# A fused convolution and feed-forward block: the first matmul wholly in seven products, in two passes, with its sums and its output moved between engines and groups

## The chip, the cores and the metric

The kernel runs on 1 core of one Trainium2 chip. The metric is device microseconds (us) of one execution. Before the change three runs took 971.06, 972.87 and 970.63 us, median 971.06 us. PE is the matrix engine, DVE the vector engine, ACT the scalar engine, POOL is GpSimd, and SP issues most loads and stores.

## The reference, cut to what matters

```python
# x: (8, 4224, 192) f32; weight: (8 heads, 7 taps)
w = softmax(weight, axis=-1)
y[b, s, h*24 + g] = sum over k of w[h, k] * x_pad[b, s + k, h*24 + g]   # 6 zero rows ahead
mu, var = mean and variance of y over its 192 channels
yn = (y - mu) / sqrt(var + 1e-6) * g_ln
out = y + maximum(yn @ w_ch1, 0) @ w_ch2          # w_ch1: 192 x 768, w_ch2: 768 x 192
```

The mean and g_ln are folded into w_ch1 at the start. The factor 1/sqrt(var + 1e-6) is positive, so it goes through the maximum and is applied to the result of the second matmul.

## The kernel before, in words

**Groups.** The 33,792 rows are cut into 18 groups (line 70). Groups 0 to 2 are smaller and take the plain path; groups 3 to 17 have 16 rows on each of 128 partitions, and these "mixed" groups are nearly the whole run. A group goes through the same steps, spread over three turns of the main loop (line 912). Its x is loaded two turns ahead (`load_x`). Behind it the convolution `y` is made: tap 0 by ACT (`first_tap`, line 383), tap 1 by ACT into a scratch tile `tb` that two DMAs of POOL add to `y` (`second_tap`, lines 394 and 397), taps 2 to 6 by DVE (`conv`, line 408, 40 instructions, one for each tap and head). DVE then turns `y` into 32x32 transposed blocks `yt` (line 419) and takes the moments (line 439, 16 instructions).

**First matmul (`up_mixed`, line 584).** The 768 columns of w_ch1 are six chunks of 128, three in the left half (e = 0) and three in the right (e = 1). `yt` is cut in quarters a11 to a22 (two halves of the rows by two halves of the channels) and w1 in quarters b11 to b22, and the four result quarters c11 to c22 come from seven products in place of eight, at the price of sums of quarters: of w1 once (`sums_of_quarters`), of `yt` in each group (`sums_of_y`, lines 574 to 578, four DVE additions). Four of the six chunks go so, two at a time, each product into one of two sets of four PSUM banks, `chain` and `other`. The remaining two (`plain`) are made with all eight. ACT copies a finished product out of PSUM (`evict`, line 607). Where a second product has to be added to a quarter (`close`), ACT copies it into a scratch tile and a DMA of POOL adds it in SBUF (line 582); only in the last group DVE adds it straight from PSUM (line 614). The scratch tiles are taken from the pools of `tb` and of `cs`.

**Second matmul (`down_fast`, line 743).** Again seven products, here called A to G in their order, each of three columns and each column evicted by ACT (line 768). E, F and G read sums of hidden quarters that DVE makes between them (`half_sum`, line 727, nine instructions), and B reads a sum made by `lower_sum` (line 736, three instructions). Results gather in the tile `cs`; one of the two last additions is a DMA of POOL (`close_by_dma`), the other is DVE's (line 822).

**Output.** `finish_fast` transposes `cs` back into the tile `ot` (line 824, six instructions), at the end of the group's own turn. In the next group's first matmul ACT scales the 16 rows of `ot` by the root (line 849), and POOL issues two DMAs that add rows 0 to 7 and 8 to 15 to the output in DRAM (`add_to_out`, line 856), where SP has stored `y` before.

**What sets the order.** The schedule is manual: each engine runs its instructions in the order of the program text, and waits are put in where one instruction needs another. The pools of `yt`, `tb`, `cs`, `ot` and of the hidden tile have one buffer each (lines 106 to 112), so a new tile of such a pool waits until every reader of the last one is done, a DMA that reads it included. `x` and `y` have two buffers. DMAs that POOL issues share one queue.

Of the kernel before, what the change touches and what calls it, by code (L numbers as in the profile page):

```python
# [16 lines left out]
def kernel(  # L17
# [200 lines left out]
    def split_words(raw, mant, power, clamp=nc.vector):  # L218
        hi = raw[:, :, 1]
        nc.vector.tensor_single_scalar(mant.bitcast(U32), hi, 0xFFFFF, op=ALU.bitwise_and)  # L220
        nc.scalar.activation(mant.bitcast(F32), mant, AF.Relu, scale=2.0**-20, bias=1.0)
        nc.vector.tensor_scalar(
            out=power.bitcast(U32), in0=hi, scalar1=20, scalar2=0x7FF,
            op0=ALU.logical_shift_right, op1=ALU.bitwise_and,
        )
        clamp.tensor_scalar(  # L226
            out=power, in0=power, scalar1=896.0, scalar2=1151.0, op0=ALU.max, op1=ALU.min
        )
        nc.scalar.activation(power, power, AF.Relu, scale=float(1 << 23), bias=low)  # L229
# [46 lines left out]
    w1sums = consts.tile([P, 4, CH, PAIR * P], F32, name="w1sums")  # L276
# [88 lines left out]
    split_words(*words_a, nc.gpsimd)  # L365
    split_words(*words_b, nc.gpsimd)
    tap_matrices(range(3, K))
    join_words(w1f[:, 0:2].rearrange("p s f -> p (s f)"), *words_a, ga)
    join_words(w1f[:, 2], *words_b, gb)
# [143 lines left out]
    def rows_of_tiles(banks, left, right, first=True, last=True):  # L513


        chunks, w = right.shape[2] // P, left.shape[1] * left.shape[3]
        for c in range(left.shape[2]):
            for i in range(chunks):
                for q in range(NQ):
                    rows = slice(C * q, C * q + C)  # L520
                    nc.tensor.matmul(  # L521
                        banks[:, q, i * w : i * w + w], right[rows, c, P * i : P * i + P],
                        left[rows, :, c, :], start=(first and c == 0 and i == 0),
                        stop=(last and c == left.shape[2] - 1), skip_group_check=chunks > 1,
                    )
# [22 lines left out]
    def quarters_of_w1():  # L548
        return [
            w1[:, CH * k : CH * k + CH, P * f : P * (f + PAIR)] for k in range(2) for f in (0, FC)  # L550
        ]

    def sums_of_quarters(dst, b11, b12, b21, b22):

        for v, a, b in ((0, b12, b11), (1, b22, 0), (2, b12, b22), (3, b21, 1)):
            a, b = (dst[:, u] if isinstance(u, int) else u for u in (a, b))
            nc.vector.tensor_tensor(dst[:, v], a, b, op=ALU.subtract)
# [10 lines left out]
    def sums_of_y(g):  # L568

        room = upool.tile([P, 3 * HJ * CH * C], F32, tag="ys", name=f"ysums{g}")  # L570
        room = room.rearrange("p (v j c t) -> p v j c t", v=3, c=CH, t=width(g))
        ysums[g] = s1, s2, s3 = [room[:, v] for v in range(3)]
        a11, a12, a21, a22 = quarters_of_y(g)
        nc.vector.tensor_tensor(s1, a21, a22, op=ALU.add)
        nc.vector.tensor_tensor(s2, s1, a11, op=ALU.subtract)
        nc.vector.tensor_tensor(s3, a21, a11, op=ALU.subtract)
        yield
        nc.vector.tensor_tensor(s2, a12, s2, op=ALU.subtract)
        yield
# [4 lines left out]
    def up_mixed(g, last_sum):  # L584
# [4 lines left out]
        assert groups[g][2] == 2 * HJ and PAIR * W == 512  # L589
# [3 lines left out]
        b11, b12, b21, b22 = quarters_of_w1()  # L593
        s1, s2, s3 = ysums[g]
        (c11, c12), (c21, c22) = [
            [a[:, h, e, 0:PAIR].rearrange("p f q j t -> p f q (j t)") for e in range(2)]
            for h in range(2)
        ]
# [5 lines left out]

        def evict(banks, dst, relu=False, i=slice(0, PAIR)):
            src = banks.rearrange("p q (f w) -> p f q w", w=W)[:, i]
            nc.scalar.activation(dst, src, AF.Relu) if relu else nc.scalar.copy(dst, src)  # L607

        def close(c, banks, part, i=slice(0, PAIR)):


            if last:
                src = banks.rearrange("p q (f w) -> p f q w", w=W)[:, i]
                nc.vector.tensor_tensor(c[:, i], c[:, i], src, op=ALU.add)
                return
            evict(banks, part, i=i)
            whole = "p f q w -> p (f q w)"
            add_by_dma(c[:, i].rearrange(whole), part.rearrange(whole))

        def plain(f, banks):  # L620
            rows_of_tiles(banks, yt[g][:, 0 : 2 * HJ], w1[:, :, f * P : f * P + P])
            evict_up(g, f, banks)


        chain, other = take_set(), take_set()
        turn[0] += 4
        done = groups[g - 1][2]
        rooms = parts(bpool, "tb"), parts(cpool, "cs")
        first, second = (r[:, 0:PAIR] for r in rooms)
# [8 lines left out]

        rows_of_tiles(chain, a11, b11, True, False)
        evict(chain, c11)  # L640
        rows_of_tiles(other, a12, b21)
        close(c11, other, first)
        rows_of_tiles(chain, s2, w1sums[:, 1], False, False)
        evict(chain, c21)
        act_scales(0, 1)
        taps_of_next(2, 3)
        next(last_sum)
# [8 lines left out]
        rows_of_tiles(other, s3, w1sums[:, 2], True, False)  # L656
        evict(other, c22)
        act_scales(1, 2)
        rows_of_tiles(chain, s1, w1sums[:, 0], False, False)
        close(c22, chain, second)  # L660
        act_scales(2, 3)
        rows_of_tiles(other, a22, w1sums[:, 3], False)
        for i, room in enumerate(rooms):
            close(c21, other, room[:, PAIR : PAIR + 1], slice(i, i + 1))
        act_scales(3, 4)
        rows_of_tiles(chain, s2, b22, False)
        evict(chain, c12, True)
        nc.scalar.activation(c11, c11, AF.Relu)
        act_scales(4, 7)
        taps_of_next(3, 6)  # L670
        taps_of_next(6, K, heads=(0, H // 2))
        plain(PAIR, other)
        nc.scalar.activation(c22, c22, AF.Relu)
        if not last:
            scale(g - 1, 7, 10)
            add_to_out(g - 1, 0, 8)
        lower_sum(g, (PAIR,))
        lower_sum(g, range(PAIR))
        taps_of_next(6, K, heads=(H // 2, H))
        plain(PAIR + FC, chain)  # L680
        if last:

            rest = a[:, 1, 0, 0:PAIR, :, fast[g] :]
            for f in range(PAIR):
                nc.scalar.activation(rest[:, f], rest[:, f], AF.Relu)
        else:
            scale(g - 1, 10, done)
            add_to_out(g - 1, 8, done)
# [54 lines left out]
    def down_fast(g):  # L743
# [7 lines left out]
        part = cpool.tile([P, CH, NFAST * T], F32, tag="part", name=f"part{g}")[:, :, 0:w]  # L751
        part = part.rearrange("p c (j t) -> p c j t", t=t)

        parts = [part, a[:, 1, 0].rearrange("p f q j t -> p (f q) j t")[:, 0:CH]]
# [22 lines left out]
        def close_by_dma(c, part):  # L777
            add_by_dma(*(v.rearrange("p c j t -> p c (j t)") for v in (c, part)))

# [5 lines left out]
        taps_behind = [1, 4, 4, 7, 0, 0]  # L785
        product(0, a[:, 0, 0], b[0], c11, True)
        some_taps(taps_behind[0])
        product(1, a[:, 1, 0], w2sums[:, 2], c22, True)
        some_taps(taps_behind[1])
        product(1, a[:, 1, 1], w2sums[:, 3], parts[0], False)  # L790
        some_taps(taps_behind[2])
        product(1, a[:, 0, 1], b[2], None, True)
        some_taps(taps_behind[3])
        if g + 1 < NG:
            transpose(g + 1)
            moments(g + 1, 0, EARLY)
# [8 lines left out]
        product(0, a[:, 1, 1], w2sums[:, 1], c21, False)  # L805
        if g + 1 == NG:
            finish_fast(g, 0, flat, cs, parts)
        else:
            close_by_dma(c21, parts[0])
        some_taps(taps_behind[4])  # L810
        product(0, a[:, 0, 0], w2sums[:, 0], parts[1], False)
        some_taps(taps_behind[5])
        product(0, a[:, 0, 1], b[3], c12, False)
        some_taps(len(todo))
        return flat, cs, parts

    def finish_fast(g, half, flat, cs, parts):
        n = fast[g]
        ot = ots[g] if half else out_tile(g)
        if half or g + 1 == NG:  # L820
            fresh = cs[:, CH * half : CH * half + CH, 1]
            nc.vector.tensor_tensor(fresh, fresh, parts[half], op=ALU.add)
# [88 lines left out]
    store_y(0)  # L911
    for g in range(NG):
# [3 lines left out]
        if mixed:  # L916
            up_mixed(g, later)
        else:
            up(g)
        if not fast[g]:  # L920
# [13 lines left out]
            if g == 1:  # L934
                finish(0)
                root(0)
                sums_of_quarters(w2sums, *quarters_of_w2())
# [3 lines left out]
            elif g == 2:  # L941
                sums_of_quarters(w1sums, *quarters_of_w1())
                later = sums_of_y(3)
# [6 lines left out]
        parts = down_fast(g)  # L950

        if not last:
            moments(g + 1, EARLY)
            if g + 1 in MIXED:
                later = sums_of_y(g + 1)
                next(later)
            for half in range(2):
                finish_fast(g, half, *parts)
# [4 lines left out]
        else:  # L963
            finish_fast(g, 1, *parts)
            add_and_store(g, slice(0, fast[g]))
            down(g)
            finish(g)
# [30 lines left out]
```

## Time and profile before

| what | value |
|---|---|
| time of the profiled execution | 971.06 us |
| its span, first to last instruction | 969.3 us |
| around the span | 1.8 us |
| start of the first matmul of groups 3, 4, 5, ... 17 | 122.5, 178.7, 234.7, ... 906.4 us: 56.0 us each |
| of these: first matmul, second matmul | 28.64 and 27.33 us |
| from group 17's first matmul to the span's end | 62.8 us |

The span is what lies between the first and the last recorded instruction. Rows of the timeline give the start, the time from the first start to the last end, engine, line, operation, tiles, shape and count, and in brackets the engine's idle time before it and what ended that. In a table of stretches an engine's entry is its busy time and its number of instructions.

### The profile page before, as it was taken

The numbers are of one execution on the slowest core, as the hardware profiler recorded it, in microseconds if no ns is written. First come the engines' busy times: TensorE is split into PE (matmuls) and PEld (weight loads), VectorE is DVE, ScalarE is ACT, GpSimd is POOL, SyncE is SP. The second block draws the span as 40 slices with busy tenths as digits, with TensorE's granted clock in tenths as the row PEclk, the third lists the DMA queues.
The fourth block names the chain that finished last, engine by engine and source line by source line (L and its number), as shares of the span: only waits on it lengthen the run. The fifth ranks groups of instructions, "written<-read, shape, count | busy, mean of one in ns | idle before, by whom it ended". The sixth has DMA issues, their size and how long they took to land.

```text
span 969.3 us, 36017 instructions
## 1 busy us (share of the span) xinstructions
PE 956.9 (99%) x16194; PEld 672.8 (69%) x16194; DVE 870.0 (90%) x1487; ACT 640.3 (66%) x1014; POOL 205.3 (21%) x357
## 2 busy tenths in 40 slices
PE   6999999999999999999999999999999999999997
PEld 6886585857658585766758586675857667685767
DVE  6999999898998989899997989899798989989837
ACT  5725677585867858595876858587685858675351
POOL 3005310411123111411114011321104111130400
PEclk9999999999999999999999999999999999999999
DMA  8243888687796969789696978969697886766121
GB/s 205 93 134 123 173 199 234 127 161 230 147 271 127 247 124 190 206 156 271 128 247 125 194 198 152 266 132 249 132 216 176 147 255 133 178 123 111 28 59 68
DMA packets 29960, 163.17 MB, mean 168 GB/s; under 512 B 3567, under 2 KB 9839, under 8 KB 22126
## 3 DMA queue, kind: packets, MB, share of 16 engines
q0 software_dynamic: 22704, 97.53, 53.7%
q1 hardware_dynamic: 6798, 63.34, 17.0%
q8 instruction: 127, 2.08, 0.9%
q14 instruction: 27, 0.22, 0.1%
q10 hardware_dynamic: 304, 0.00, 0.0%
HBM read 38.95 MB, written 50.33 MB: 92 GB/s over the span
## 4 chain that ended last, share of the span: by engine, by line
PE 98%; DMA 1%; DVE 1%; POOL 0%; ACT 0%; issue 0%; SPq 0%
PE ps L521 49%; PE ps L762 41%; PE ps L707 6%; DMA room<-in_moe_w_ch_dram 1%; PE ps L320 1%; POOL room L226 0%; PE ps L344 0%; PE ps L349 0%; DVE y L863 0%; PE ps L329 0%; PE ps L332 0%; DVE room L245 0%; DVE room L237 0%; ACT room L229 0%; DVE ot L888 0%; DVE room L220 0%
## 5 line engine op out<-in xcount | busy, mean ns | idle before, releaser
L408 DVE SCALAR_TENSOR_TENSOR y<-xg,taps,y 128x384 f32<-128x384 f32 (+3 forms) x734 | 368.2, 581 | 1.4 <-issue 0.9
L521 PE MATMUL ps<-yt,w 32*128 32x256 f32 (+3 forms) x3744 | 287.7, 458 | 0.0
L521 PEld LDWEIGHTS ps<-yt,w 32*128 32x128 f32 x3744 | 187.9, 185 | 91.2 <-issue 81.0
L762 PE MATMUL ps<-room,w2sums 128*32 128x256 f32 (+1 forms) x4320 | 233.9, 375 | 0.0
L762 PEld LDWEIGHTS ps<-room,w2sums 128*32 128x32 f32 x4320 | 142.4, 110 | 86.0
L762 PE MATMUL ps<-room,w 128*32 128x256 f32 (+1 forms) x3240 | 179.9, 375 | 0.0
L727 DVE TENSOR_TENSOR room<-room 128x1024 f32<-128x1024 f32 (+1 forms) x135 | 151.4, 1196 | 9.7 <-ACT part L768 9.7
L762 PEld LDWEIGHTS ps<-room,w 128*32 128x32 f32 x3240 | 105.2, 110 | 73.4 <-ACT ot L849 10.6
L768 ACT COPY cs<-ps 128x256 f32<-128x256 f32 (+1 forms) x180 | 63.0, 366 | 97.7 <-PE ps L762 97.0
L607 ACT COPY room<-ps 128x2048 f32<-128x2048 f32 x45 | 84.0, 1867 | 55.1 <-PE ps L521 54.4
L521 PE MATMUL ps<-ysums,w1sums 32*128 32x256 f32 x2160 | 119.6, 374 | 0.0
L521 PEld LDWEIGHTS ps<-ysums,w1sums 32*128 32x128 f32 x2160 | 110.5, 185 | 6.4 <-ACT parts_tb L607 0.3
L824 DVE STREAM_TRANSPOSE ot<-cs 128x512 f32<-128x512 f32 (+1 forms) x90 | 55.9, 672 | 56.8 <-DMA cs<-part 34.5
L511 ACT ACTIVATE room<-ps 128x2048 f32<-128x2048 f32 (+3 forms) x46 | 71.3, 1549 | 33.6 <-PE ps L521 33.6
L849 ACT ACTIVATE ot<-ot,r 128x192 f32<-128x192 f32 x232 | 90.9, 448 | 0.0
L383 ACT ACTIVATE y<-xg,taps 128x384 f32<-128x384 f32 (+3 forms) x141 | 73.3, 589 | 6.9 <-DMA out_dram<-y 6.9
L856 POOL DMA_DIRECT2D out_dram<-ot x40 | 34.2, 1083 | 198.7 <-ACT ot L849 137.1
L439 DVE BATCH_NORM_STATS2 st<-y 128x6 f32<-128x192 f32 x264 | 71.0, 342 | 0.0
L397 POOL DMA_DIRECT2D y<-tb x28 | 24.6, 1036 | 176.2 <-ACT cs L768 172.8
L736 DVE SCALAR_TENSOR_TENSOR room<-room 128x1024 f32<-128x1024 f32 (+1 forms) x45 | 51.5, 1201 | 8.4 <-ACT room L509 7.6
L394 ACT ACTIVATE tb<-xg,taps 128x384 f32<-128x384 f32 x112 | 58.1, 604 | 0.0
L419 DVE STREAM_TRANSPOSE yt<-y 128x3072 f32<-128x3072 f32 (+3 forms) x19 | 56.2, 2957 | 1.9
(104 smaller groups left out, 796.3 us busy)
## 6 DMA issues: line engine op xcount, KB each, us to landing
xg<-in_x_dram SPq DMA_DIRECT2D x15, 2112.0 KB, 15.2
out_dram<-ot POOLq DMA_DIRECT2D x29, 768.0 KB, 8.0
y<-tb POOLq DMA_DIRECT2D x28, 768.0 KB, 9.5
out_dram<-y SPq DMA_DIRECT2D x13, 1536.0 KB, 10.5
room<-parts_tb POOLq DMA_DIRECT2D x14, 1024.0 KB, 7.4
room<-parts_cs POOLq DMA_DIRECT2D x14, 1024.0 KB, 7.1
room<-parts_tb POOLq DMA_DIRECT2D x14, 512.0 KB, 9.2
room<-parts_cs POOLq DMA_DIRECT2D x14, 512.0 KB, 10.8
```

Source lines behind the costliest of these rows:

```text
L383: nc.scalar.mul(y[g][:, 0:n, cs], xg[g][:, 0:n, cs], taps[:, h, 0:1])
L394: nc.scalar.mul(tb[g][:, 0:n, cs], xg[g][:, 1 : 1 + n, cs], taps[:, h, 1:2])
L408: nc.vector.scalar_tensor_tensor(out=y[g][:, 0:n, cs], in0=t[:, k : k + n, cs], scalar=taps[:, h, k : k + 1], in1=y[g][:, 0:n, cs], op0=AL ...
L439: nc.vector.bn_stats(out=sums[g][:, j, :], in_=y[g][:, j, :])
L511: nc.scalar.activation(dst, src, AF.Relu)
L521: nc.tensor.matmul(banks[:, q, i * w : i * w + w], right[rows, c, P * i : P * i + P], left[rows, :, c, :], start=(first and c == 0 and i = ...
L607: nc.scalar.activation(dst, src, AF.Relu) if relu else nc.scalar.copy(dst, src)
L707: nc.tensor.matmul(bank[C * q : C * q + C, 0:w], w2[:, f, C * c : C * c + C], left, start=(f == 0), stop=(f == NF - 1),)
L727: nc.vector.tensor_tensor(a[:, *dst, f], a[:, *left, f], a[:, *right, f], op=op)
L762: nc.tensor.matmul(dst[C * q : C * q + C, 0:w], right[:, f, C * c : C * c + C], left[:, f, q], start=(first and f == 0), stop=(f == FC - 1 ...
L768: nc.scalar.copy(to[:, c], dst[:, 0:w].rearrange("p (j t) -> p j t", t=t))
L849: nc.scalar.mul(ots[g][:, j, :], ots[g][:, j, :], rstd[g][:, j : j + 1])
```

## The change

The first matmul makes all six chunks with seven products, in two passes: pass one has one chunk of each half (7 products of 12 matmuls), pass two the other two (7 products of 24). The sums of w1 now span three chunks and are arranged so that one is kept in w1 itself. Two of the four sums of `yt` go to GpSimd, right behind the transpose; a fourth one overwrites a quarter of `yt`. In pass two the last addition to c21 is DVE's, from PSUM. In the second matmul the addition by DMA becomes DVE's, and `finish_fast` of a group stands in the next group, behind pass one and ahead of the taps. The scaling of `ot` is spread over pass two and the second matmul of the next group (`ending`), and the ACT taps of `first_tap` and `second_tap` are given out as 4, 6 and 6 behind the products C, D and E. At the start the bound on the exponents of w_ch1 goes from GpSimd to DVE.

```diff
-        clamp.tensor_scalar(
+        nc.vector.tensor_scalar(
             out=power, in0=power, scalar1=896.0, scalar2=1151.0, op0=ALU.max, op1=ALU.min
         )
...
+    def sums_of_y(g, engine):
...
+        engine.tensor_tensor(s3, a21, a11, op=ALU.subtract)
+        engine.tensor_tensor(s2, s3, a22, op=ALU.add)
         yield
-        nc.vector.tensor_tensor(s2, a12, s2, op=ALU.subtract)
+        nc.vector.tensor_tensor(s4, a12, s2, op=ALU.subtract)
+        nc.vector.tensor_tensor(a21, a21, a22, op=ALU.add)
...
+            def close(self, c, banks, part=None):
+                if part is None or last:
+                    nc.vector.tensor_tensor(c, c, self.seen(banks), op=ALU.add)
+                    return
+                self.evict(banks, part)
...
+        X, Y = take_set(), take_set()
+        one, two = Pass(PAIR, FC, X, Y), Pass(0, PAIR, Y, X)
+        room1 = parts(bpool, "tb")
+        p = one
+        p.product(X, a11, p.b11, True, False)
+        p.evict(X, p.c11)
+        p.product(Y, a12, p.b21)
+        p.close(p.c11, Y, room1[:, 0:1])
+        p.product(X, s2, p.t[0], False, False)
+        p.evict(X, p.c21)
+        p.product(Y, s3, p.t[1], True, False)
+        p.evict(Y, p.c22)
+        p.product(X, s1, p.b12, False, False)
+        p.close(p.c22, X, room1[:, 1:2])
+        p.product(Y, a22, p.t[2], False)
+        p.close(p.c21, Y, room1[:, 2:3])
+        p.product(X, s4, p.b22, False)
+        p.evict(X, p.c12, True)
+        next(ahead)
+        p = two
+        room2 = parts(cpool, "cs")
+        room3 = parts(bpool, "tb")
...
+        p.product(Y, s1, p.b12, False, False)
+        taps_of_next(2, 5)
+        taps_of_next(5, 6, heads=(0, H // 2))
+        p.close(p.c22, Y, room3[:, 0:PAIR])
+        p.product(X, a22, p.t[2], False)
+        taps_of_next(5, 6, heads=(H // 2, H))
+        p.relu(p.c11)
+        p.close(p.c21, X)
+        p.product(Y, s4, p.b22, False)
+        p.evict(Y, p.c12, True)
         lower_sum(g, (PAIR,))
         lower_sum(g, range(PAIR))
+        taps_of_next(6, K)
+        def ending(step):
+            if step == 0:
+                two.relu(two.c22)
+            if last:
+                return
+            cuts = [min(j, done) for j in (3, 6, 10, 13, J)]
+            if step < len(cuts) - 1:
+                scale(g - 1, cuts[step], cuts[step + 1])
+            if step == 1:
+                add_to_out(g - 1, 0, 8)
+            if step == 3:
+                add_to_out(g - 1, 8, done)
...
         product(0, a[:, 0, 0], b[0], c11, True)
+        ending(0)
         product(1, a[:, 1, 0], w2sums[:, 2], c22, True)
+        ending(1)
+        product(1, a[:, 1, 1], w2sums[:, 3], c21, False)
+        some_taps(4)
         product(1, a[:, 0, 1], b[2], None, True)
+        some_taps(6)
         if g + 1 < NG:
             transpose(g + 1)
-            moments(g + 1, 0, EARLY)
+            sums = sums_of_y(g + 1, nc.gpsimd)
+            next(sums)
+            moments(g + 1)
...
-        product(0, a[:, 1, 1], w2sums[:, 1], c21, False)
-            close_by_dma(c21, parts[0])
+        product(0, a[:, 1, 1], w2sums[:, 1], parts[0], False)
+        some_taps(6)
+        ending(2)
         product(0, a[:, 0, 0], w2sums[:, 0], parts[1], False)
+        some_taps(len(todo))
+        ending(3)
         product(0, a[:, 0, 1], b[3], c12, False)
+        if g + 1 < NG:
+            next(sums)
```

`next(ahead)` runs `finish_fast(g - 1, half, ...)` for both halves, the two calls that stood behind `down_fast`.

## The prediction

> **What bounds the kernel now.** I read the chain that ended last, then a table of stretches of one group each, then the timelines of DVE, POOL and ACT over the same stretch, then the transfers' issues and landings. The chain:
>
> ```profile
> PE 98%; DMA 1%; DVE 1%; POOL 0%; ACT 0%; issue 0%; SPq 0%
> ```
>
> PE sets the end. Of two neighbouring groups:
>
> ```profile
> 458.55:514.55 56.00, 56.00 (x940) 38.32 (x936) 51.54 (x83) 40.24 (x62) 11.25 (x14) 1.00 0.81 188
> 514.55:570.57 56.02, 56.02 (x941) 41.73 (x937) 51.29 (x83) 40.29 (x62) 12.79 (x25) 1.00 0.82 188
> ```
>
> The columns are length, PE, weight loads, DVE, ACT, POOL, clock, DMA share, GB/s. PE is busy for all of 56.0 us at the full clock; DVE has work for 51.5 us of it, so only 4.5 us to spare, and the DMA engines are 81% busy. The spare DVE time is one wait:
>
> ```profile
> 567.93 0.94 DVE L574 TENSOR_TENSOR ysums<-yt 128x768 f32<-128x768 f32 x1
> 568.91 0.96 DVE L575 TENSOR_TENSOR ysums<-ysums,yt 128x768 f32<-128x768 f32 x1
> 569.79 0.95 DVE L576 TENSOR_TENSOR ysums<-yt 128x768 f32<-128x768 f32 x1
> 574.94 1.90 DVE L824 STREAM_TRANSPOSE ot<-cs 128x512 f32<-128x512 f32 x3 [4.20 <-DMA cs<-part]
> 576.76 0.92 DVE L822 TENSOR_TENSOR cs<-cs,room 128x768 f32<-128x768 f32 x1
> 577.78 1.90 DVE L824 STREAM_TRANSPOSE ot<-cs 128x512 f32<-128x512 f32 x3
> 579.60 4.28 DVE L408 SCALAR_TENSOR_TENSOR y<-xg,taps,y 128x384 f32<-128x384 f32 x8
> ```
>
> DVE waits 4.2 us for the DMA that adds `part` to `cs`; the taps of the next group stand behind that wait. And POOL's transfers:
>
> ```profile
> 542.49 0.86 POOL L856 DMA_DIRECT2D out_dram<-ot  x1 [8.97 <-ACT ot L849]
> 547.58 0.86 POOL L856 DMA_DIRECT2D out_dram<-ot  x1 [4.22 <-ACT cs L768]
> 561.39 1.75 POOL L397 DMA_DIRECT2D y<-tb  x2 [12.94 <-ACT cs L768]
> 563.57 1.28 POOL L582 DMA_DIRECT2D cs<-part  x1 [0.43 <-ACT cs L768]
> 578.30 0.91 POOL L582 DMA_DIRECT2D room<-parts_tb  x1 [13.45 <-ACT parts_tb L607]
> ```
>
> The last output transfer leaves at 547.6 and lands 9.5 us later, at 557.1, which is 17.8 us before DVE wants `ot` at 574.9. The two `tb` transfers leave at 561.4 and land at 568.4 and 572.8; ACT wants their scratch room at 576.1, and in 15 groups waited only once:
>
> ```profile
> ACT parts_tb L607 <- DMA y<-tb: 1.2, 1, 1.2
> ```
>
> Both one-buffer tiles are free in time now. The change moves both their last readers later and their next writers earlier.
>
> **PE.** A product of pass two is one of today's: 24 matmuls, 2.59 us (7 take 18.24 with the entry). One of pass one has half, 1.30 us. Today: 18.24 + 10.40 (two plain chunks) = 28.64; after: 21 x 1.295 + 0.1 = 27.3. The second matmul keeps its 27.33. So PE needs 54.6 us in place of 56.0; over 15 groups 20.1 us are saved if nothing waits. Pass one's ring is tight: ACT starts 0.25 after a product ends, copies 128x1024 in 1.02 (row of L607 with that shape) and PE resumes 0.05 after a release (L614 ends at 914.31, PE starts at 914.36), 1.32 against 1.30: with the restart about 0.1 every second product, 0.3 a group.
>
> **DVE.** Off: two sums, 1.9 us. On: an addition to c21 from PSUM, 2.29 (L614, 128x2048), and one in `finish_fast`, 0.92. 51.5 becomes 52.8, still under 54.6. By busy time the change fits. What decides is the order.
>
> **POOL's sums.** The only two-input rows of POOL are tiny: 128x16 0.22 us, 128x32 0.25, which is 1.9 ns an element and 1.65 us for 768; L226, one input of 768, took 2.78. I take 2.0 each, 3.3 to 5.6 for both. They start behind the transpose, beside 4.1 us of moments, and DVE wants them 14 us later: nothing, unless they collide with DVE's nine half sums. That they can collide is shown: L457 to L459 took 0.92 to 1.01 beside L574 to L576, against 0.25 elsewhere. The Trainium skill, "GPSIMD Engine Reference", Engine selection and Key points, speaks against this step: two-input work is about twice slower there than on VectorE, and GpSimd contends with DVE instructions of two SBUF inputs; by it (an estimate from that page, twice the 0.95 of L574) the two take 3.8 us, the same answer.
>
> **The order: loop one, `ot`.** In the changed kernel's instruction lists the first transpose of `finish_fast(g - 1)` waits for both output transfers of group g - 2. The second follows the scaling of rows 13 to 15, which ACT does behind F of group g - 1, so it leaves about 2 us ahead of that group's end at best. Everything of DVE's group is queued behind that transpose: 40 taps, c21, `lower_sum`, transpose, moments, half sums; and E needs the half sums. From landing to landing, 0 being when `ot` is free:
>
> - six transposes and an addition 4.67 (519.03 to 523.70 in the timeline): 4.7
> - 32 taps, 28 took 14.82: 16.9, at 21.6
> - c21 from PSUM 2.3; `lower_sum` 3.4; 8 taps 4.2; transpose 3.4; 16 moments 4.1 (10 took 2.57): at 39.1
> - three half sums 3.4; E's first column ends 0.4 behind the third, two columns more take 2.6: E ends at 45.6
> - ACT's last copy of E 0.25 + 0.37, six taps 3.2 (eight took 4.16), POOL starts 0.3 later: `tb` leaves at 49.7
> - the two `tb` transfers land after 6.1 and 9.8 (group 3's, with no x load beside them): at 59.5
> - the output transfer, issued at about 52.8, is behind them in POOL's queue. These land one behind another: `tb`, `tb`, `cs` at 568.43, 572.78, 574.81. 768 KB take 3.7 to 4.4; I take 4.2: at 63.7.
>
> So a group takes 63.7 us where it took 56.0. With the landings beside an x load (7.0, 11.4, +4.35) it is 65.4. If the output transfer weren't held by `tb`: F ends at 49.5, copies 0.6, three scalings 1.1, 0.3, and alone it lands in 7.0: 58.5, the lower end of this loop.
>
> **Loop two, `tb`.** Pass one's second eviction writes a room of the `tb` pool, which now is wanted 2.9 us into the group rather than 5.6, and waits for both `tb` transfers; they leave later too, 4.1 us behind E's end where now they leave 1.2 ahead of it (561.4; E ends at 562.6). From landing: eviction 1.0, four products 5.5, six of pass two 15.6, c21 2.5, then 3.4 + 4.2 + 3.4 + 4.1, E's end 6.5 later, `tb` leaves 4.1 after that, lands in 9.8: 60.3 us. Loop one is longer, so it sets the pace and this wait is hidden in it.
>
> **The rest.** The start: L226 took 2.78 + 1.48 on POOL, DVE's own of 128x1152 takes 0.76; the chain ends about 1.0 us sooner. Group 3 has no `finish_fast`, but `tb` lands at 128.5, 6.0 us into it, so PE's fourth product starts 3.2 us late and c21 follows: about 60.2. The last group closes on DVE in both versions and saves about 1.0.
>
> **The sum.** The profiled execution took 971.06 us (span 969.3 and 1.8 around it), which is also the median. Groups 3 to 16 took 783.9. 971.06 - 783.9 + 60.2 + 13 x 63.7 - 2.0 = **1073.5 us**, slower.
>
> **Rivals.**
>
> - Loop two alone (the output transfer isn't held up by `tb`): 13 x 60.3, 1029 us. For: three queued transfers are all I have to show that they follow one another. Chance 0.18.
> - Loop one with a lone transfer and `tb` early: 13 x 58.5, 1006 us. Chance 0.06.
> - Faster: PE stays the bound, 971 - 20.1 - 2.0 + 4.5 for pass one's ring = 953 us. It decides by one landing: PE wants the first half sum 42.9 us into a group, DVE gives it 40.3 after `ot` is free, so the second output transfer has to land within 2.6 us of the group's start, 4.5 us after it leaves. The least of this size is 6.9. For it: only busy times. 0.05.
> - Heavier: POOL's sums run into the half sums and each waits for the other, or the transfers land as beside an x load, 66 us a group and over: 1103 us. 0.09.
> - The forecast, 62.5 to 65.4 us a group: 1058 to 1096 us. 0.62.
>
> **The numbers.** The range runs from the second loop's time, less some, to the forecast's upper end and a bit: 1020 to 1100 us; about 0.18 is left out. What this kernel's measurement can tell from no change is about 0.2%, 2 us. Faster 0.04, same 0.01 (both from the rival in which PE stays the bound), slower 0.95.
>
> **What would show it.** Right: groups 62 to 65 us apart; on DVE an idle time of some 10 us ahead of the first transpose into `ot`, ended by the transfer `out_dram<-ot`; on ACT a wait of `parts_tb` for `y<-tb`; PE waiting ahead of E for a half sum. DVE's busy time still near 52.8 a group. Wrong: groups of 54.6 us and no idle time on PE, or a DVE that waits for POOL's sums in place of a transfer.

## The result, and the profile after

The changed kernel takes **1088.08 us** (median of 1086.92, 1087.69, 1088.47 and 1089.79); the kernel before took 971.96 us on the same chip. The ratio is 1.1196, interval 1.1173 to 1.1220: slower by 12%. The prediction had 1073.5 us, range 1020 to 1100. The profiled run took 1087.69 us, with a span of 1085.9.

From the start of group 4's first matmul (182.50 us) to group 17's (1023.04) a group takes 64.66 us; before it was 55.98. The page's busy times, its chain, and the transposes into `ot`:

```profile
PE 977.6 (90%) x17274; PEld 740.3 (68%) x17274; DVE 893.3 (82%) x1491; ACT 685.6 (63%) x1083; POOL 230.5 (21%) x383
...
PE 6%; DVE 2%; ACT 0%; issue 0%
...
L857 DVE STREAM_TRANSPOSE ot<-cs 128x512 f32<-128x512 f32 (+1 forms) x90 | 55.9, 672 | 152.5 <-DMA out_dram<-ot 104.1
```

PE has no longer the whole span. The chain that carried the reading of before is of no use here: its shares come to 8%, because it could be followed back only over the last stretch. The last line does its work: DVE was idle for 152.5 us ahead of these transposes, 9.2 to 12.2 us in each of 13 groups. Two groups in the table of stretches:

```profile
506.14:570.60 64.46, 56.66 (x1013) 42.98 (x1009) 52.71 (x83) 43.35 (x67) 12.68 (x16) 1.00 0.71 166
570.60:635.47 64.87, 57.98 (x1012) 42.17 (x1009) 53.16 (x83) 43.45 (x67) 15.85 (x26) 0.97 0.70 165
```

No column is full: PE 56.7 of 64.5, DVE 52.7, the DMA engines 0.71 where they had 0.81. So the loss is in waits and not in work. The waits, with their total, count and longest:

```profile
DVE ot L857 <- DMA out_dram<-ot: 104.1, 9, 12.2
DVE ot L857 <- ACT room L616: 46.9, 4, 11.9
ACT parts_tb L616 <- DMA y<-tb: 44.8, 14, 5.1
PE ps L521 <- ACT parts_tb L616: 42.2, 28, 4.5
```

The first two are one wait: in 4 groups the profile puts it down to a copy on ACT that ended within 0.2 us behind the landing, but in all 13 groups DVE starts 0.1 to 0.2 us after the output transfer has landed. The third is loop two's wait, and the fourth what PE sees of it. DVE's timeline from one wait to the next:

```profile
516.02 1.90 DVE L857 STREAM_TRANSPOSE ot<-cs 128x512 f32<-128x512 f32 x3 [11.60 <-DMA out_dram<-ot]
...
520.69 16.99 DVE L408 SCALAR_TENSOR_TENSOR y<-xg,taps,y 128x384 f32<-128x384 f32 x32
537.59 2.28 DVE L622 TENSOR_TENSOR room<-room,ps 128x2048 f32<-128x2048 f32 x1
...
550.85 4.21 DVE L439 BATCH_NORM_STATS2 st<-y 128x6 f32<-128x192 f32 x16
554.98 10.29 DVE L764 TENSOR_TENSOR room<-room 128x1024 f32<-128x1024 f32 x9
...
580.46 1.90 DVE L857 STREAM_TRANSPOSE ot<-cs 128x512 f32<-128x512 f32 x3 [11.58 <-DMA out_dram<-ot]
```

Between the two waits DVE runs without a gap: taps, c21, lower sums, taps, transpose, moments, half sums. And GpSimd's timeline in that stretch:

```profile
551.10 1.83 POOL L575 TENSOR_TENSOR ysums<-yt 128x768 f32<-128x768 f32 x1 [0.86 <-PE ps L797]
553.01 1.84 POOL L576 TENSOR_TENSOR ysums<-ysums,yt 128x768 f32<-128x768 f32 x1
565.53 1.77 POOL L397 DMA_DIRECT2D y<-tb  x2 [10.67 <-ACT tb L394]
568.40 0.87 POOL L889 DMA_DIRECT2D out_dram<-ot  x1 [1.09 <-ACT ot L882]
```

The two `tb` transfers land at 571.68 and 576.41, the output transfer behind them at 580.33, which is 11.9 us after its issue; 0.13 us later DVE starts. That is loop one of the prediction, closed.

### The profile page after: what moved, and what is told of

Same layout as the page of the kernel before. It is cut to its first block, busy times and chain, and to the rows that moved or that the text cites. A ratio compares the mean times of both kernels' runs of the same rounds, so it can differ in the third digit from the quotient of the medians.

```text
span 1085.9 us, 38303 instructions
## 1 busy us (share of the span) xinstructions
PE 977.6 (90%) x17274; PEld 740.3 (68%) x17274; DVE 893.3 (82%) x1491; ACT 685.6 (63%) x1083; POOL 230.5 (21%) x383
## 5 line engine op out<-in xcount | busy, mean ns | idle before, releaser
L521 PE MATMUL ps<-yt,w 32*128 32x256 f32 (+2 forms) x4104 | 240.5, 381 | 0.0
L521 PEld LDWEIGHTS ps<-yt,w 32*128 32x128 f32 x4104 | 208.5, 188 | 25.8 <-issue 7.0
L797 PEld LDWEIGHTS ps<-room,w 128*32 128x32 f32 x3240 | 112.9, 110 | 100.5 <-issue 17.9
L857 DVE STREAM_TRANSPOSE ot<-cs 128x512 f32<-128x512 f32 (+1 forms) x90 | 55.9, 672 | 152.5 <-DMA out_dram<-ot 104.1
L616 ACT COPY room<-ps 128x1024 f32<-128x1024 f32 (+1 forms) x90 | 129.6, 1440 | 75.9 <-PE ps L521 75.9
L521 PE MATMUL ps<-ysums,w1sums 32*128 32x256 f32 x2160 | 135.0, 395 | 35.7 <-ACT parts_tb L616 35.7
L616 ACT COPY parts_tb<-ps 128x1024 f32<-128x1024 f32 (+1 forms) x56 | 68.5, 1223 | 57.4 <-DMA y<-tb 44.8
L583 POOL DMA_DIRECT2D room<-parts_tb x56 | 48.3, 862 | 249.9 <-ACT parts_tb L616 177.2
L629 ACT ACTIVATE room<-room 128x1024 f32<-128x1024 f32 (+1 forms) x60 | 87.5, 1486 | 1.4 <-DMA room<-parts_tb 1.4
L521 PE MATMUL ps<-ysums,w 32*128 32x256 f32 x1080 | 65.8, 382 | 6.5 <-ACT parts_tb L616 6.5
L803 ACT COPY room<-ps 128x256 f32<-128x256 f32 (+1 forms) x90 | 30.2, 364 | 60.6 <-PE ps L797 57.4
```

Source lines behind the costliest of these rows:

```text
L521: nc.tensor.matmul(banks[:, q, i * w : i * w + w], right[rows, c, P * i : P * i + P], left[rows, :, c, :], start=(first and c == 0 and i = ...
L583: nc.gpsimd.dma_start(out=dst, in_=src, accum_op=ALU.add)
L629: nc.scalar.activation(c, c, AF.Relu)
L797: nc.tensor.matmul(dst[C * q : C * q + C, 0:w], right[:, f, C * c : C * c + C], left[:, f, q], start=(first and f == 0), stop=(f == FC - 1 ...
L803: nc.scalar.copy(to[:, c], dst[:, 0:w].rearrange("p (j t) -> p j t", t=t))
L857: nc.vector.transpose(ot[:, 0:n, C * c : C * c + C], flat[:, c].rearrange("p (j t) -> p j t", t=C))
```

## The experiments

The loops keep the prediction's names: loop one goes through `ot`, loop two through `tb`. The theory was that loop one sets the pace and loop two stands right behind it; the main rival, that the transfers only fill time which DVE's and GpSimd's work needs anyway. A group's time is the mean of groups 4 to 16 of the profiled run. Intervals are 95%. On the chips of these runs the kernel before took 974.8 to 975.4 us, so ratios are compared.

| run | edit to the changed kernel | us | ratio to before, interval | a group, us |
|---|---|---|---|---|
| changed kernel | none | 1088.08 | 1.1196, 1.1173 to 1.1220 | 64.66 |
| 1 | pass one's room not from `tb` | 1093.22 | 1.1195, 1.1175 to 1.1215 | 65.36 |
| 2 | `tb` sent ahead of the output | 1043.59 | 1.0700, 1.0670 to 1.0730 | 61.00 |
| 3 | output sent early | 1114.78 | 1.1432, 1.1393 to 1.1471 | 66.04 |
| 4 | as 3, but behind GpSimd's sums | 1073.96 | 1.1011, 1.0959 to 1.1063 | 63.33 |
| 5 | GpSimd's sums on DVE | 1141.54 | 1.1704, 1.1680 to 1.1728 | 68.26 |
| 6 | 1 and 3 | 1044.08 | 1.0704, 1.0687 to 1.0720 | 61.43 |
| 7 | 1, 3, six taps ahead of c21 | 1013.71 | 1.0388, 1.0368 to 1.0407 | 58.88 |
| 8 | 1, 4, `tb` and scaling sooner, taps | 996.97 | 1.0238, 1.0208 to 1.0268 | 57.57 |
| 9 | as 8, ACT's order tightened | 1023.05 | 1.0502, 1.0487 to 1.0516 | 59.55 |
| 10 | as 9, a memset moved | 973.81 | **0.9979**, 0.9967 to 0.9991 | 55.63 |
| 11 | as 10, sums on DVE | 980.76 | 1.0060, 1.0047 to 1.0073 | 56.22 |
| 12 | kernel before, bound on DVE | 973.82 | 0.9989, 0.9980 to 0.9998 | 55.98 |

**1. Loop two's wait taken away.** The scratch room of pass one is carved out of regions of the hidden tile that are unused then.

```diff
-        room1 = parts(bpool, "tb")
+        room1 = [a[:, 0, 1, 0:1], a[:, 0, 1, 1:2], a[:, 1, 1, 0:1]]
```

> The changed kernel with the scratch room of pass one carved out of regions of the hidden tile that are unused at that time, so that pass one no longer waits for the tb pool; no work is left out. Theory (loop one sets the pace): the wait of parts_tb for y<-tb at pass one's second eviction goes, PE's first 9 us of a group are smooth, and the time stays: 1088 us, within 4, groups 64.3 to 65.0 us apart. Rival, loop two (tb) sets the pace: the group falls with it, to below 62 us, 1050 us or less.

The time stayed: 1.1195 against 1.1196. The wait of `parts_tb` for `y<-tb` at that eviction is gone from the table of waits, and DVE's wait for the output transfer is as large as before:

```profile
DVE ot L858 <- DMA out_dram<-ot: 141.4, 12, 13.2
```

Loop two alone doesn't set the pace. (The profiled run was the longest of its four, and in it GpSimd's sums run into the half sums, which take 10.3 to 11.6 us; its groups are a little over the changed kernel's.)

**2. The queue term by itself.** All 16 tap instructions of ACT stand ahead of E's copies, so that `tb` leaves before the output.

```diff
         some_taps(4)
         product(1, a[:, 0, 1], b[2], None, True)
-        some_taps(6)
+        some_taps(12)
...
-        some_taps(6)
         ending(2)
```

> The changed kernel with all 16 tap instructions of ACT ahead of E's copies (4 behind C, 12 behind D) in place of six of them behind E, so that the tb transfers leave ahead of the output transfer by more than their own time; no work is left out. Theory (loop one holds because the output transfer lands behind the two tb transfers in GpSimd's queue): the output transfer lands about 7 us after its issue in place of 11.9, a group takes 58.6 to 59.6 us in place of 64.7, ratio 1.04 to 1.06. Rival, the output transfer is slow by itself or held by something else than the queue: ratio 1.11 or more.

In the group shown the output transfer now lands 7.05 us after its issue (550.48 to 557.53) in place of 11.9; over the 13 groups it is 5.6 to 10.0 us against 11.3 to 12.5, though the second `tb` transfer is still under way at the issue (here until 553.09). So what made it late was the two transfers ahead of it. The ratio fell from 1.12 to 1.07. The group missed its forecast by 1.4 us and more. Part of that shows in GpSimd's timeline:

```profile
542.33 1.75 POOL L397 DMA_DIRECT2D y<-tb  x2 [10.42 <-ACT room L803]
543.43 5.21 POOL L575 TENSOR_TENSOR ysums<-yt 128x768 f32<-128x768 f32 x1
...
550.48 0.89 POOL L889 DMA_DIRECT2D out_dram<-ot  x1
```

GpSimd works in order: its two sums, ready at 532.5, now stood behind the `tb` issue, which waits for ACT. They started 10.9 us late, ran beside DVE's half sums, the first took 5.21 us in place of 1.83, and the output transfer went out when they were done. Of four neighbouring groups from 490.7 us on, the two with the full clock take 60.4 and 60.0 us, the two with 0.97 granted 62.8 and 61.5.

**3. Loop one taken away, first try.** The rest of the rows is scaled behind B, and the second output transfer issued there.

```diff
-            cuts = [min(j, done) for j in (3, 6, 10, 13, J)]
+            cuts = [min(j, done) for j in (3, 6, J)]
...
-            if step == 3:
                 add_to_out(g - 1, 8, done)
```

> The changed kernel with the second half of a group's output scaled and sent behind product B of the next group rather than behind F; no work is left out. Theory (loop one, ot, sets the pace and loop two, tb, stands close behind it): DVE's idle time ahead of the first transpose into ot, ended by the output transfer, goes; what is late next is the wait of parts_tb for y<-tb, so a group takes 60.3 us by the prediction's terms, 61.4 with the second tb landing at 10.9 us as the changed kernel's trace has it, in place of 64.7: 1031 to 1046 us. Rival, DVE's and GpSimd's work is the pace and the transfer only fills the time: no change, 1088 us. Rival, tb does not bind at all once ot is free: 57 us a group or less, 990 us or less.

This was a clear miss: no theory had it slower, and it was, by 1.143 against 1.120. Its timelines of DVE and GpSimd:

```profile
521.10 17.02 DVE L408 SCALAR_TENSOR_TENSOR y<-xg,taps,y 128x384 f32<-128x384 f32 x32 [3.08 <-issue]
...
560.61 0.87 POOL L888 DMA_DIRECT2D out_dram<-ot  x1 [1.89 <-ACT cs L802]
561.18 2.17 POOL L575 TENSOR_TENSOR ysums<-yt 128x768 f32<-128x768 f32 x1
562.33 12.81 DVE L763 TENSOR_TENSOR room<-room 128x1024 f32<-128x1024 f32 x9
563.43 2.69 POOL L576 TENSOR_TENSOR ysums<-ysums,yt 128x768 f32<-128x768 f32 x1
```

DVE's wait for `ot` is gone, as meant. But the transfer's issue waits for ACT's scaling until 560.6 and holds GpSimd's sums, ready at 558.2, behind it. They run beside the half sums, and now both are slower: the second sum takes 2.69 us in place of 1.84, nine half sums 12.81 in place of 10.29, and E waits for them. The first line shows a second arm of loop two that I had not counted: the taps read `y`, to which `tb` is added, so DVE itself waits for the second `tb` transfer (it landed at 521.02), under the label "issue". It has time to spare: behind these taps DVE waits 6.81 us for PE ahead of c21.

**4. The same without that collision.** Only the second issue is moved, behind the sums; `rest_of_output` holds it.

```diff
             next(sums)
+            rest_of_output(g - 1)
             moments(g + 1)
```

> The run with the output sent early again, but with the second output transfer issued behind GpSimd's two sums in place of ahead of them; no work is left out. Theory (sent early, the transfer holds GpSimd's sums until they run beside DVE's half sums, 12.8 us in place of 10.3 for nine; and behind that, loop two sets the pace): the half sums are back at 10.3 us, E ends 2.8 us sooner, a group takes 61 to 62.5 us, ratio to the kernel before 1.07 to 1.09. Rival, the early transfers themselves cost it, beside the load of x: no better than the run before it, ratio 1.13 or more.

The cause holds: in ten of the 13 groups the half sums are back at 10.3 to 10.4 us (10.29 at 551.87), and the ratio falls from 1.143 to 1.101. The size was missed: 63.3 us a group and not 61 to 62.5. In the other three groups the half sums still take 10.9 to 11.8 us, and groups differ with the granted clock, the third column from the right:

```profile
439.35:503.44 64.09, 59.31 (x1012) 43.09 (x1008) 53.12 (x85) 43.16 (x67) 16.85 (x28) 0.95 0.70 167
...
566.44:627.91 61.47, 56.49 (x1013) 41.07 (x1009) 53.12 (x85) 43.19 (x67) 16.87 (x28) 1.00 0.73 174
```

The second of these, at the full clock, takes 61.5 us, which is loop two: from one landing of the second `tb` transfer (573.39) the next two leave 50.5 us later, as forecast, and the second lands 11.0 after that. With 0.95 granted a group takes 64.1, with 2.8 us more PE time; another at the full clock, with half sums of 11.83 us, takes 63.0.

**5. GpSimd's sums undone.** The two sums stand on DVE again.

```diff
-            sums = sums_of_y(g + 1, nc.gpsimd)
+            sums = sums_of_y(g + 1, nc.vector)
```

> The changed kernel with the two sums of y on DVE in place of GpSimd; no work is left out. Theory (GpSimd's sums lie beside the moments and cost nothing, and DVE's row is in loop one): a group takes 1.8 us more, 66.4 us, ratio 1.143. Rival, the sums on GpSimd hold DVE up by more than they take off it: the ratio stays at 1.12 or falls.

In the changed kernel the sums are a gain: without GpSimd a group takes 3.6 us more. That is twice the 1.8 expected, and the other half is the clock. PE's timeline at E:

```profile
517.46 0.64 PE L797 MATMUL ps<-room,w2sums 128*32 128x256 f32 x8 [2.61 <-DVE room L764]
...
519.73 8.74 PE L797 MATMUL ps<-room,w2sums 128*32 128x256 f32 x128 [0.49 <-DVE room L764]
```

And of the changed kernel:

```profile
556.25 0.64 PE L797 MATMUL ps<-room,w2sums 128*32 128x256 f32 x8 [0.53 <-DVE room L764]
...
558.52 7.11 PE L797 MATMUL ps<-room,w2sums 128*32 128x256 f32 x128 [0.50 <-DVE room L764]
```

DVE's sums, 1.9 us, make E wait 2.61 us; the changed kernel's E waited 0.53. Then the same 128 matmuls of E and F that took 7.11 us there take 8.74, and E is on loop one: 1.9 + 1.6 is 3.5 us. The granted clock is 0.50 from 519.7 to 523.1 us, which is E. For the whole group it is 0.95, and for its neighbours too:

```profile
465.33:533.44 68.11, 59.55 (x1012) 44.10 (x1008) 54.65 (x85) 43.36 (x67) 12.18 (x24) 0.95 0.67 157
```

**6 and 7. Both loops together.** Run 6 has edits 1 and 3; run 7 also has six of the eight instructions of tap 6 ahead of c21's addition.

```diff
+        taps_of_next(6, K, heads=(0, 6))
         p.close(p.c21, X)
...
-        taps_of_next(6, K)
+        taps_of_next(6, K, heads=(6, H))
```

> Both edits together: the output sent early and pass one's room in the hidden tile; no work is left out. Theory: both loops through transfers are gone. What is late next is DVE's order: the addition to c21, lower sum, eight taps, transpose, moments and half sums still stand in one row between product Q6 of pass two and E, so a group takes about 57 us, 980 to 995 us in all. Rival, the two loops were only covers for DVE's and GpSimd's work: 61 us a group or more, 1040 us or more. Rival, PE becomes the bound at once: 54.7 us a group, 955 us.

> Both edits, and six of the eight instructions of tap 6 ahead of the addition to c21 in place of behind the lower sum, so that DVE's row between c21 and E is 3.2 us shorter; no work is left out. Theory: PE becomes the bound, 54.7 to 55.5 us a group, 953 to 966 us, which would beat both kernels. Rival, DVE's row is not what is late once the transfers are gone (GpSimd's sums or a lower granted clock are): as with both edits alone, 57 us a group, 980 us or more.

Both missed, and the rivals' numbers held: 61.4 and 58.9 us a group. Run 6 carries edit 3's collision (half sums 12.49 us) and DVE's wait for `tb` ahead of the taps (4.58 us in the group looked at). In nine of run 7's 13 groups the collision takes a third form, in the timelines of DVE and GpSimd:

```profile
518.85 10.29 DVE L765 TENSOR_TENSOR room<-room 128x1024 f32<-128x1024 f32 x9
...
519.75 11.10 POOL L575 TENSOR_TENSOR ysums<-yt 128x768 f32<-128x768 f32 x1
...
532.80 0.96 DVE L578 TENSOR_TENSOR ysums<-yt,ysums 128x768 f32<-128x768 f32 x1 [2.66 <-POOL ysums L576]
```

DVE keeps its speed and GpSimd gets nothing until the half sums end: one sum takes 11.10 us, DVE then waits 2.66 for the second, and `tb` is issued late behind both.

**8 to 10. A version with all the waits gone.** Run 8 joins edits 1 and 4 with 14 taps of ACT ahead of E's copies and the scaling spread as 6, 5 and 5 rows.

> All remedies together: pass one's room in the hidden tile; scaling 6 rows in pass two, 5 behind A and 5 behind B, the first output transfer behind A and the second behind GpSimd's sums; 14 of the 16 tap instructions of ACT ahead of E's copies; six instructions of tap 6 ahead of the addition to c21. No work is left out. Theory: PE is the bound again, 54.7 to 55.8 us a group, ratio 0.98 to 0.995, faster than both kernels. Rival, DVE's work with its waits for the tb landings stays the bound: 57 us a group or more, ratio 1.01 or more.

57.6 us: the rival's number. PE was busy for 55.9 of the 57.2 us of a group; it waited for late copies of ACT, and DVE 2.3 us for `tb`. Run 9 makes a group's first taps one group earlier, in ACT's gaps behind E and F, and so loads x one turn earlier in the program.

> The run with all remedies, with ACT's order tightened: the first taps of a group made one group earlier, in ACT's gaps behind E and F, so that tb leaves 45 us into a group in place of 51; the two ReLUs of pass one no longer in one gap; 8 rows scaled ahead of B's copies and 8 behind them; the load of x issued in the turn before. No work is left out. Theory (what is left over PE's 54.6 us are ACT's late evictions and DVE's 2.3 us wait for tb): 55.3 to 56.5 us a group, ratio 0.985 to 1.005. Rival (pass one's ring and DVE's 53.2 us of work hold the group wherever ACT's work is put): 57 us or more, ratio 1.015 or more.

A miss as a whole, but made of two kinds of group that alternate, here in the table of stretches:

```profile
485.77:541.01 55.24, 55.24 (x1012) 42.33 (x1008) 49.60 (x79) 43.16 (x67) 15.21 (x12) 1.00 0.66 161
541.01:607.05 66.04, 58.49 (x1012) 43.25 (x1008) 56.48 (x89) 43.27 (x67) 17.14 (x32) 0.92 0.84 195
```

GpSimd's timeline shows what spoils the second kind:

```profile
530.04 1.05 POOL L161 MEMSET xg<- 1x1152 f32 x1 [18.39 <-DMA xg<-in_x_dram]
```

I had moved an instruction on GpSimd without counting it: every second group clears the padding of x, and that memset waits for the whole load. The output transfer, the sums and `tb` stood behind it. Run 10 puts it behind the `tb` issue:

```diff
-            load_x(g + 3)
+            load_x(g + 3, clear=False)
...
                 send_tb(g + 2)
+            if g + 3 < NG:
+                clear_pad(g + 3)
```

> The run before it, with the memset of the padding of x behind the tb transfers in GpSimd's row in place of ahead of the output transfer: every second group has this memset, and it waits for the whole load of x while the output transfer, the sums and tb stand behind it. No work is left out. Theory (that memset is all that separates the groups of 64 to 66 us from their neighbours of 55.24): all groups 55.2 to 55.6 us, ratio 0.985 to 0.995, faster than both kernels. Rival (the groups of 55.24 only catch up after a late one, and in a row they fall back to DVE's pace): 57 us or more, ratio 1.015 or more.

Two of its groups in the table of stretches:

```profile
461.79:517.04 55.25, 55.25 (x1013) 42.43 (x1009) 52.91 (x84) 43.29 (x67) 18.77 (x22) 1.00 0.82 195
...
572.77:630.45 57.68, 55.67 (x1012) 43.04 (x1008) 54.73 (x86) 43.21 (x67) 21.03 (x28) 1.00 0.81 193
```

PE is the bound again, as in the first row (eight of the 13 groups take 55.24 to 55.34 us); a few groups, as in the second, still wait. Both expectations missed: not all groups came to 55.2 to 55.6 us, and the ratio lies between the two that were named. This version is faster than the changed kernel by 11% (0.9979 / 1.1196 = 0.891), but than the one before only by 0.2%, which is at the edge of what can be told.

**11. The sums once more, with PE as the bound.**

> The same with the two sums of y on DVE in place of GpSimd. No work is left out. Theory (with PE as the bound, DVE's 53.2 us of work and the 1.9 us of these sums come to 55.1 us of a 55.2 us group, and half sums 1.9 us later than E wants them): 56 to 57.5 us a group, ratio 1.00 to 1.025, so that here the sums on GpSimd earn their place. Rival (DVE has room enough, and GpSimd's sums were worth nothing): the same as without this edit.

As expected: the groups take 56.2 us each with the sums on DVE, 1.0 more than run 10's groups without a wait, and the ratio is 1.006. On GpSimd, and started in time, the sums earn their place; without that there is no lead over the kernel before.

**12. The start alone.** The kernel before, with the bound on the exponents on DVE.

> The kernel before with one part of the change alone: the bound on the exponents of w_ch1 on DVE in place of GpSimd. No work is left out. The prediction's step: the start's chain ends about 1.0 us sooner, ratio 0.999. Rival: behind it the load of x is late next, as the changed kernel's 1.6 us wait for it has it, and nothing is gained: ratio 1.000 to 1.001, the first group's first matmul within 0.7 us of where it was.

The ratio is 0.9989: 1.1 us sooner, between 0.2 and 2.0, as the prediction had it. The profile shows the step, though not its gain: from the arrival of w_ch1 on DVE to PE's first matmul with it the chain takes 5.95 us (9.59 to 15.54) where it took 6.97 (7.59 to 14.56), but in this execution w_ch1 arrives 2.0 us later, and group 0's first matmul begins at 30.11 us and not at 27.07.

## Why the prediction was right, point by point

- **PE bound before, waits after: right.** PE's own need was forecast at 54.6 us and 0.3 for pass one's ring. Where nothing waits (run 10) a group is 55.24: pass one takes 9.61 us (517.04 to 526.65 in its PE timeline) where 7 x 1.295 is 9.07, so the ring costs 0.5 and not 0.3. (The least output transfer before took 6.76 us, not the 6.9 named there; the rival that stayed with PE needed 4.5.)
- **DVE's and GpSimd's work: right.** 52.8 us forecast for DVE, 52.7 measured; 2.0 us for a sum on GpSimd, 1.83 and 1.84 measured, beside the moments and at no cost, with room for a collision only when they start later.
- **Loop one: right, step by step, but for one term.** From the landing at 515.83, half sums begin at 39.15 (forecast 39.1) and `tb` leaves at 49.7 (49.7). The mis-sized term is the landing of the second `tb` transfer: 10.9 us after the first's issue, where I took 9.8 from group 3, a group with no load of x beside it. The 11.4 from a group with one was nearer, but not for that reason: in the changed kernel the load has landed (562.04) before `tb` leaves (565.53), and still the second landing comes after 10.2 to 12.1 us in groups 4 to 16. In the kernel before the last pair, without a load beside it, took 11.6; so 9.8 was the low end of a spread, whose cause stays open. The output transfer lands 3.9 behind it (4.2). Together 64.5 us in this group, 64.66 in the mean, against 63.7: over 13 groups 12.5 of the 14.2 us by which the profiled run missed.
- **The queue: right.** It was the open point of the forecast, from three transfers only. Run 2 shows it: 7.05 us with only the end of the second `tb` transfer ahead, 11.9 behind both, and always in the order of issue. Whether it is the queue itself or the DMA engines that they share, no run tells apart.
- **Loop two: right, as a cover.** Forecast 60.3 (its terms, as rounded there, come to 60.1) and hidden. Taking its wait away gains nothing (run 1); with loop one gone it is the pace (run 4), 61.5 us at the full clock. I had one of its two arms, the one that sets the pace; the other is DVE's taps, which read `y`, with 5.4 us to spare in that group.
- **A lone transfer with `tb` early: 58.5 forecast, 58.1 to 61.1 measured** in run 2's five groups at the full clock, 59.9 in the mean, where GpSimd's late sums held the issue up.
- **The heavier rival's mechanism exists, but hardly in the changed kernel's order.** There one group of 13 shows it, with half sums of 10.74 us. The sums run into the half sums as soon as they start a little later: in three groups of run 4, in runs 1 and 9, and most in runs 2, 3, 6 and 7.
- **The start: right in size** (run 12), though the profiled run shows the first group 0.7 us later than before: its chain is 1.1 us sooner (13.43 against 14.56), and then PE waits 1.56 us for the load of x. In the profiles of the other runs of the changed kind group 0's first matmul begins at 29 to 33 us, so this part varies by more than the edit is worth.
- **The last group: wrong by 1.0.** 62.8 us from its first matmul to the end, as before. In the trace its first matmul takes 28.60 us, 28.99 before and not 1.3 less, with 9.97 in pass one; the second matmul up to the plain columns takes 19.20, 18.82 before. Why was not tried and stays open. Group 3 took 59.3, 0.9 less than forecast.

The clock adds little in the changed kernel itself: its groups with 1.00 granted take 64.4 to 65.1 us, those with 0.97 take 63.9 to 64.9, the one with 0.95 takes 65.3. It costs time where the slowed matmuls lie on the loop, as in run 5.

A second buffer for `ot` should cut loop one without moving anything. It was not tried, and whether the tile fits beside the rest is not shown.

## What to carry to other kernels

Busy times said that the change fits, with 54.6 us for PE and 52.8 for DVE; the time came from following a one-buffer tile round, from the landing that frees it to the issue of the transfer that frees it next, through every engine and every queue between. An engine that works in order makes a wait of each instruction put ahead of others: in runs 3 and 9 one moved issue or memset on GpSimd cost more than the edit gained, and in runs 2, 6 and 7 it took back a part. And before such a change it is worth asking what it could bring at best: here run 10, with most of the waits gone, won 2 us of 975.

## What the runs showed of the hardware

GpSimd and DVE get in each other's way, and not in one form only: a GpSimd sum of 128x768 took 1.83 us beside the moments, 2.16 where the issue of a transfer on GpSimd still ran when it began (505.90 us in run 8), and 2.69, 5.21 or 11.10 us beside the half sums, while nine half sums took from 10.29 to 14.5 us. The Trainium skill, "GPSIMD Engine Reference", Specifications, names this: the SBUF interfaces are shared with VectorE, with contention where DVE has two SBUF inputs. The runs agree, and add that it may be either engine that pays.

PE's waits can cost twice. In run 5 waits of 2.61, 0.50 and 0.49 us end at 519.73 us; the granted clock is 0.50 from 519.7 to 523.1, for 3.4 us, and 128 matmuls take 8.74 us in place of 7.11. After waits of 2.11 and 0.50 us the same work took 8.68 us in run 6 and 7.11 in run 3. The Trainium skill, "TensorE: Matmul & The Clock Gate", What's actually happening, says that the clock is halved after an idle window of some 3.4 us and that the windows run freely, so that they don't start with the wait. One window at half the clock loses 1.7 us (an estimate from that page) beside the 1.6 measured, and free windows would account for the same waits costing something once and nothing another time. The waits that cost here were shorter than a window, while waits of 3.74 and 3.71 us in run 4 (ended at 574.56 and 636.00) left the clock at 1.00; what share of idle time is enough these runs don't show.
